# First squares of A issued later, pair 1's A groups sooner, one exchange of pair 2 later

## The chip, the cores and the metric

The kernel runs on one core of a Trainium2 chip. The metric is the device time of one execution in microseconds (us), as a median of several runs. TensorE is called PE (PEld where it loads weights), VectorE DVE, ScalarE ACT, GpSimd POOL. SyncE (SP) computes nothing: it issues nearly all DMAs and waits for semaphores, strictly in the order of its program. "SPq" in a row is that issuing.

## The reference

The input x has 8 sequences of 4096 rows with 192 columns. Each of 8 heads owns 24 columns and has 7 weights, which go through a softmax; a causal convolution over 7 rows is taken with them. Its result, 32768 rows of 192, goes through a gated feed-forward block with 1536 hidden units:

```
w = softmax(weight);  c[s] = sum_k w[head, k] * x[s - 6 + k]
g = c @ w_gate;  out = (g * sigmoid(g)) * (c @ w_val) @ w_out
```

## The kernel before, in words

**Tiling.** The 32768 rows are 64 blocks of 512 rows, two blocks to a pair, 32 pairs. The hidden units are 12 chunks of 128. The kernel's main loop goes over blocks and, inside, over chunks; its counter `at` numbers the chunks of the whole run, 0 to 767, so block n begins at chunk 12n and pair q at chunk 24q. For each chunk PE forms `gate` (L546) and `val` (L547) in PSUM, ACT applies the activation (L551, tile `silu`), DVE multiplies (L553, tile `h`), and PE multiplies `h` by the output weights (L558, tile `acc`). These output products run about a block behind: 8 matmuls ("pieces") per chunk. `gate` has two PSUM buffers, `val` three, `acc` one; ACT empties `acc` (L596) at two chunks of each block (in block 1 at chunks 16 and 22), and SP stores the result (L588). One output bank is summed in two passes. The second pass must start after the first, and this order is kept by an empty instruction on SP (`mark`, L443): PE's first piece of the second pass waits until SP has come to it.

**Convolution.** Block 0 and block 1 (pair 0) are convolved by PE in the opening, as matmuls with a banded matrix (L334). Block 1's are the calls `lateA` (chunks 2 and 4) and `lateC` (chunk 6); ACT copies the sums to `foldA1` and `foldC1`, and SP exchanges their lower and upper 64 partitions with two DMAs each (`exchange`, L657: `swapA` in chunk 4, `swapC` in chunk 6). Every chunk of block 1, the first (chunk 12) included, reads `foldA1`, `foldC1`, `swapA1` and `swapC1`, the last one last.

All later pairs are convolved by ACT, DVE and POOL. SP loads x as 32 by 32 squares (`emit_load`, L103) into `sqA` (channels 0 to 127, 1024 rows; parts 0 and 1, two DMAs each) and `sqB` (channels 128 to 191; parts 2 and 3). DVE transposes (`emit_turn`, L114) into `xtA` and `xtB`. A pair has three groups of 512 columns: g0 is the first half of A, g1 is B, g2 the second half of A. In a group ACT forms one product into a PSUM tile `run` (L473) and one or two more into tiles `t` (L466), DVE adds one or two taps (L483), POOL forms two or three products (L488), adds everything (L495) and writes the result `xc` (L501). SP then exchanges the halves of `xc` into `xs` with two DMAs (`swap`, L449 and L450), and PE reads both.

**Order.** It is written out by hand. `at_chunk(c, f)` puts f behind chunk c's own work; what is put at the same chunk runs in the order in which it was registered. `plan_group` puts one group's steps at given chunks: turn, start (ACT's `run`), ACT taps, DVE taps, POOL taps, join (POOL's adds and `xc`) and swap. For pair 1 these come from `PLAN["opening"]`, for pairs q from 2 on they are offsets to 24q from `PLAN["start"]`, `"swap"` and so on; the swaps of pair 2 stand at chunks 42 (g0), 35 (g1) and 53 (g2). Every engine executes its own instructions in this order, so a waiting instruction holds back all behind it on that engine.

Pair 1's squares are in four portions. Right after PE's first matmul of the band matrix (L310) SP issues the four loads of B and the first halves of A, four DMAs. The second halves of A follow at chunk 9.

Of the kernel before, what the change touches and what calls it, by code (L numbers as in the profile page):

```python
# [11 lines left out]
PLAN = dict(  # L12
    start=(-16, -24, -8), turn=-2,
    acts=((3, 5), (2, 4), (2, 4)), dves=(1, 3), pool=4, join=5, npool=(2, 2, 3),
    swap=(10, 11, 13),
    load=((2, -47), (3, -40), (0, -34), (1, -28)),
    opening=(
# [3 lines left out]
    ),  # L21
    gate=2, val=3, lead=4, third=(2, 11),
)
# [3 lines left out]
def kernel(  # L27
# [31 lines left out]
    n_pairs = NT // (2 * TB)  # L59
# [21 lines left out]

    def emit_load(q, part, half=None):
        head = q % ppb == 0
        if part == 2 and not half:
            squares[q, "A"] = headA if head else xpool.tile(
                [P, HIST + 2 * TB], fp32, tag="sqA", name="sqA"
            )
            squares[q, "B"] = headB if head else xpool.tile(
                [P, HIST + TB], fp32, tag="sqB", name="sqB"
            )  # L90
        for k in range(2):
            quad = 2 * (part % 2) + k
            if part < 2:
                tile_, t0, n, c = squares[q, "A"], 0, 2 * TB, SQ * quad
            else:
                tile_, t0, n, c = squares[q, "B"], TB * (part % 2), TB, P + SQ * k
            skip = HIST if head and t0 == 0 else 0
            row = q * 2 * TB + t0 - HIST + skip
            n = n // SQ + 1 - skip // SQ
            if half is not None:  # L100
                first = TB // SQ + 1
                skip, row, n = ((skip, row, first), (first * SQ, row + first * SQ, n - first))[half]
            nc.sync.dma_start(  # L103
                out=tile_[quad * SQ : (quad + 1) * SQ, skip : skip + n * SQ].rearrange("p (n c) -> p n c", c=SQ),
                in_=x_flat[row : row + n * SQ, c : c + SQ].rearrange("(n p) c -> p n c", p=SQ),
            )
# [9 lines left out]
    def sync_after(ins, earlier, why="one bank, two halves of the array"):  # L116
        tc.add_manual_dep(
            ins.ins,
            earlier.ins.name,
            mybir.DependencyInfo(mybir.DependencyClass.Sync, mybir.DependencyReason.DATA),  # L120
            reason=why,
        )
# [185 lines left out]
    def repeat(part, h0):  # L308
        bank = early[("hi", "lo")[part] + "AC"[h0 // HH]]
        return nc.tensor.matmul(  # L310
            bank[0:ROWS, 0 : HH * W], left[:, part, 0:ROWS],
            pick[:, h0 : h0 + HH, :].unsqueeze(2).to_broadcast([RT, HH, W // 8, 8]),
            start=True, stop=True,
        )
# [48 lines left out]

    if n_pairs > 1:
        sync_after(nc.sync.nop(), some, "squares after x")
        for part in (2, 3, 0, 1):
            emit_load(1, part, None if part > 1 else 0)
    repeat(1, 0)
    repeat(0, HH)
    repeat(1, HH)  # L370
# [244 lines left out]
    def at_chunk(c, f):  # L615
        todo.setdefault(c, []).append(f)

    def plan_group(q, g, turn, start, acts, dves, pool, join, swap):
        made = []
        if turn is not None:  # L620
            at_chunk(turn, lambda: emit_turn(q, g))

        def step(c, f):
            def run():
                if not made:
                    made.append(Group(q, g))
                f(made[0])

            at_chunk(c, run)

        ks = iter(range(1, K))
        step(start, lambda group: group.start_d())
        for k, c in zip(ks, acts):
            step(c, lambda group, k=k: group.act_tap(k))
        ks = list(range(1 + len(acts), K))
        for k, c in zip(ks, dves):
            step(c, lambda group, k=k: group.dve_tap(k, k == len(acts) + len(dves)))
        for k in ks[len(dves) :]:
            step(pool, lambda group, k=k: group.pool_tap(k))
        step(join, lambda group: group.join())  # L640
        step(swap, lambda group: group.swap())
# [39 lines left out]
    if n_pairs > 1:  # L681
        for part in (0, 1):
            at_chunk(9, lambda part=part: emit_load(1, part, 1))

    if n_pairs > 1:
        for g, plan in enumerate(PLAN["opening"]):
            plan_group(1, g, *plan)
    at_chunk(4, outA)
    for q in range(2, n_pairs):
        base = 2 * NCH * q  # L690
        for part, c in PLAN["load"]:
            c = {2: 14, 3: 15, 0: 17, 1: 21}[part] if q == 2 else base + c
            at_chunk(c, lambda q=q, part=part: emit_load(q, part))
        for g in range(3):
            c = base + PLAN["start"][g]
            plan_group(
                q, g, c + PLAN["turn"], c, [c + o for o in PLAN["acts"][g]],
                [c + o for o in PLAN["dves"][: 4 - PLAN["npool"][g]]],
                c + PLAN["pool"], c + PLAN["join"],
                c + PLAN["swap"][g],  # L700
            )


# [3 lines left out]
    for n in range(2 * n_pairs):  # L707
        block = Block(n)
        for j in range(NCH):
# [6 lines left out]
            half = src.done // (2 * NCH) - 1 if units and src.done % (2 * NCH) == 0 else None  # L716
# [82 lines left out]
```

## Time and profile before

| | us |
|---|---|
| median of 3 runs (lowest, highest) | 768.93 (768.78, 769.22) |
| the profiled execution's own time | 770.07 |
| its span | 768.3 |
| PE busy | 761.8 (99%) |
| POOL, DVE, ACT busy | 668.5, 658.4, 656.8 (87%, 86%, 85%) |
| SP's DMA row (q1), share of the 16 DMA engines | 38.5% |
| POOL's DMA row (q0: the weights), same share | 1.6% |

The profile is of one execution, whose time of 770.07 us is 1.77 us above its span. All times inside the run count from the start of the span. The granted clock of PE was 1.00. PE is busy 99% of the span, so a part of the run counts only where PE idles or is slowed; matmuls are pipelined, and PE can read as busy while it runs below its rate. A row of a timeline holds start, duration, engine, line and tiles; "xN" are N instructions merged.

### The profile page before, as it was taken

The numbers are of one execution on the slowest core, as the hardware profiler recorded it, in microseconds if no ns is written. First come the engines' busy times: TensorE is split into PE (matmuls) and PEld (weight loads), VectorE is DVE, ScalarE is ACT, GpSimd is POOL, SyncE is SP. The second block draws the span as 40 slices with busy tenths as digits, with TensorE's granted clock in tenths as the row PEclk, the third lists the DMA queues.
The fourth block names the chain that finished last, engine by engine and source line by source line (L and its number), as shares of the span: only waits on it lengthen the run. The fifth ranks groups of instructions, "written<-read, shape, count | busy, mean of one in ns | idle before, by whom it ended". The sixth has DMA issues, their size and how long they took to land.

```text
span 768.3 us, 28285 instructions
## 1 busy us (share of the span) xinstructions
PE 761.8 (99%) x11035; PEld 498.5 (65%) x11035; DVE 658.4 (86%) x1051; ACT 656.8 (85%) x1187; POOL 668.5 (87%) x650
## 2 busy tenths in 40 slices
PE   8999999999999999999999999999999999999998
PEld 3866666666666666666666666666666666666666
DVE  7888888888888888888888888888888888888875
ACT  6888888888888888888888888888888888888875
POOL 7999898888998888988889988889888899888850
PEclk9999999999999999999999999999999999999999
DMA  9543344434344433444443344334444334443211
GB/s 175 106 89 88 78 89 92 90 83 87 88 86 88 91 87 79 90 91 88 87 84 90 84 88 93 87 79 88 93 87 89 83 88 85 89 95 86 61 47 54
DMA packets 255280, 67.27 MB, mean 88 GB/s; under 512 B 207919, under 2 KB 255145, under 8 KB 255145
## 3 DMA queue, kind: packets, MB, share of 16 engines
q1 hardware_dynamic: 252041, 63.47, 38.5%
q0 software_dynamic: 2800, 1.77, 1.6%
q8 instruction: 86, 1.41, 0.8%
q14 instruction: 49, 0.40, 0.2%
q10 hardware_dynamic: 304, 0.22, 0.1%
HBM read 29.64 MB, written 25.17 MB: 71 GB/s over the span
## 4 chain that ended last, share of the span: by engine, by line
PE 96%; POOL 2%; DMA 1%; SPq 0%; issue 0%; ACT 0%; POOLq 0%
PE gate L546 60%; PE acc L558 32%; PE val L547 3%; DMA w_sb<-in_moe_w_val_dram 1%; POOL t L495 1%; DMA x_sb<-in_x_dram 0%; POOL xc L501 0%; PE acc L750 0%; POOL t L488 0%; SPq L450 0%; PE acc L334 0%; PE val L750 0%; PE run L750 0%; POOL x L229 0%; ACT silu L551 0%
## 5 line engine op out<-in xcount | busy, mean ns | idle before, releaser
L553 DVE TENSOR_TENSOR h<-silu,val 128x512 f16<-128x512 f16 x768 | 508.7, 680 | 100.5 <-ACT silu L551 69.8
L551 ACT ACTIVATE silu<-gate 128x512 f16<-128x512 f32 x768 | 452.9, 594 | 100.7 <-PE val L547 93.7
L495 POOL TENSOR_TENSOR t<-t,t 128x512 f32<-128x512 f32 x310 | 393.9, 1271 | 59.4 <-ACT t L466 38.1
L546 PE MATMUL gate<-xc,w_sb 64*128 64x512 f16 x1116 | 409.7, 376 | 0.0
L547 PE MATMUL val<-xc,w_sb 64*128 64x512 f16 x1116 | 409.7, 376 | 0.0
L558 PEld LDWEIGHTS <-h 64*128 64x128 f16 x6048 | 275.9, 94 | 141.3 <-SPq L443 1.7
L546 PE MATMUL gate<-xs,w_sb 64*128 64x512 f16 x1116 | 360.0, 376 | 0.0
L547 PE MATMUL val<-xs,w_sb 64*128 64x512 f16 x1116 | 360.0, 376 | 0.0
L558 PE MATMUL acc<-wo_sb,h 64*128 64x192 f16 x6048 | 356.4, 243 | 0.7 <-SPq L443 0.7
L546 PEld LDWEIGHTS <-w_sb 64*128 64x128 f16 x2340 | 212.3, 94 | 114.8 <-DMA w_sb<-in_moe_w_gate_dram 1.0
L547 PEld LDWEIGHTS <-w_sb 64*128 64x128 f16 x2340 | 208.3, 94 | 3.6 <-DMA w_sb<-in_moe_w_val_dram 1.7
L501 POOL TENSOR_TENSOR xc<-t,aD 128x512 f16<-128x512 f32 x93 | 118.1, 1270 | 7.3
L488 POOL TENSOR_SCALAR t<-xtA,wn 128x512 f32<-128x512 f32 x155 | 106.1, 696 | 0.7 <-DVE xtA L114 0.7
L466 ACT ACTIVATE t<-xtA,wn 128x512 f32<-128x512 f32 x124 | 88.5, 713 | 0.0
L596 ACT COPY o<-acc 128x384 f32<-128x384 f32 x126 | 60.4, 479 | 2.5
L488 POOL TENSOR_SCALAR t<-xtB,wn 128x512 f32<-128x512 f32 x63 | 43.0, 696 | 3.6 <-DVE xtB L114 3.6
L483 DVE SCALAR_TENSOR_TENSOR aD<-xtA,wn,run 128x512 f32<-128x512 f32 x62 | 45.9, 741 | 0.0
L466 ACT ACTIVATE t<-xtB,wn 128x512 f32<-128x512 f32 x61 | 43.5, 714 | 0.0
L473 ACT ACTIVATE run<-xtA,wn 128x512 f32<-128x512 f32 x62 | 42.5, 686 | 0.0
L114 DVE STREAM_TRANSPOSE xtA<-sqA 128x544 f32<-128x544 f32 (+1 forms) x48 | 34.6, 721 | 0.0
L483 DVE SCALAR_TENSOR_TENSOR run<-xtA,wn,run 128x512 f32<-128x512 f32 x31 | 23.2, 749 | 0.0
L483 DVE SCALAR_TENSOR_TENSOR run<-xtB,wn,run 128x512 f32<-128x512 f32 x31 | 23.2, 749 | 0.0
(112 smaller groups left out, 177.2 us busy)
## 6 DMA issues: line engine op xcount, KB each, us to landing
out_dram<-o SPq DMA_DIRECT2D x127, 192.0 KB, 2.0
sqA<-in_x_dram SPq DMA_DIRECT2D x92, 132.0 KB, 2.9
xs<-xc SPq DMA_DIRECT2D x186, 64.0 KB, 2.0
sqB<-in_x_dram SPq DMA_DIRECT2D x96, 68.0 KB, 2.3
headA<-in_x_dram SPq DMA_DIRECT2D x28, 128.0 KB, 2.6
headB<-in_x_dram SPq DMA_DIRECT2D x14, 68.0 KB, 2.3
headB<-in_x_dram SPq DMA_DIRECT2D x14, 64.0 KB, 2.0
w_sb<-in_moe_w_gate_dram POOLq DMA_DIRECT2D x3, 192.0 KB, 6.8
```

The costliest lines, as they stand in the source:

```text
L466: mul(parts[-1], *self.tap(k))
L473: nc.scalar.mul(self.aD, *self.tap(0))
L483: nc.vector.scalar_tensor_tensor(out=self.aD, in0=v, scalar=s, in1=run, op0=ALU.mult, op1=ALU.add)
L488: self.product(k, lambda t, v, s: nc.gpsimd.tensor_scalar(t, v, scalar1=s, scalar2=1.0, op0=ALU.mult, op1=ALU.mult), self.parts)
L495: nc.gpsimd.tensor_tensor(self.parts[0], self.parts[0], t, op=ALU.add)
L501: nc.gpsimd.tensor_tensor(xc, self.parts[0], self.aD, op=ALU.add)
L546: nc.tensor.matmul(g, w[0:DB, ca, f], a[0:DB, :], start=(i == 0), stop=(i == 2))
L547: nc.tensor.matmul(v, w[DB:P, cb, f], b[DB:P, :], start=(i == 0), stop=(i == 2))
L551: nc.scalar.activation(s, self.g.pop(j), AF.Silu)
L553: nc.vector.tensor_tensor(h, s, self.v.pop(j), op=ALU.mult)
L558: ins = nc.tensor.matmul(acc, self.h[j][r, ts(s, P)], wo_r[r, j, :], start=first and j == 0, stop=not first and j == NCH - 1, skip_group_c ...
L596: nc.scalar.copy(self.o[:, 2 * half : 2 * half + 2, :], self.acc[:, :, 0:D])
```

## The change

The change touches the first three pairs only. SP issues the first halves of pair 1's squares of A in chunk 4, behind block 1's first exchange (`outA`), and no longer in the opening. Pair 1's g0 has its steps one chunk sooner, all but the swap (chunk 20 as before). Its g2 is turned and started two chunks sooner, with ACT taps in chunks 20 and 22 (22 and 23 before), the DVE tap in 19 (21), POOL taps in 18 (20), join in 22 (23), and the swap in 31 as before. Pair 2's g2 is exchanged in chunk 56 (53 before).

```
     opening=(
-        (11, 13, (14, 15), (14, 15), 12, 15, 20),
+        (10, 12, (13, 14), (13, 14), 11, 14, 20),
         (2, 4, (8,), (4, 6), 4, 8, 14),
-        (18, 20, (22, 23), (21,), 20, 23, 31),
+        (16, 18, (20, 22), (19,), 18, 22, 31),
     ),
...
-        if part == 2 and not half:
+        if part == 2:
...
-        for part in (2, 3, 0, 1):
-            emit_load(1, part, None if part > 1 else 0)
+        for part in (2, 3):
+            emit_load(1, part)
...
     at_chunk(4, outA)
+    if n_pairs > 1:
+        for part in (0, 1):
+            at_chunk(4, lambda part=part: emit_load(1, part, 0))
...
-                c + PLAN["swap"][g],
+                c + PLAN["swap"][g] + (3 if (q, g) == (2, 2) else 0),
```

The entries of a plan are turn, start, ACT taps, DVE taps, POOL taps, join, swap. No instruction is added or taken away.

## The prediction

> **What bounds the kernel now.** I read the page first (PE busy 761.8 of 768.3 us), then the table of windows, cut at the first gate matmul of each block, to see where PE runs below its best. The columns are the stretch, its length, then busy time of PE, PEld, DVE, ACT and POOL.
>
> ```profile
> 8.50:20.90 12.40, 11.20 (x227) 5.74 (x228) 9.62 (x21) 8.59 (x17) 8.30 (x10) 1.00 1.16 168
> 20.90:33.06 12.16, 12.16 (x245) 11.80 (x243) 11.04 (x19) 9.88 (x19) 11.00 (x12) 1.00 0.66 119
> 33.06:45.07 12.01, 12.01 (x174) 8.08 (x170) 10.81 (x18) 10.90 (x21) 11.37 (x13) 1.00 0.35 76
> 45.07:57.65 12.58, 11.92 (x174) 7.85 (x170) 9.71 (x17) 10.73 (x20) 12.02 (x13) 1.00 0.50 103
> 57.65:69.38 11.73, 11.73 (x173) 7.43 (x170) 10.76 (x18) 9.89 (x19) 11.17 (x12) 1.00 0.30 70
> ```
>
> From block 4 on each block takes 11.73 us and PE waits for nothing. Blocks 1, 2 and 3 take 0.43, 0.28 and 0.85 more. So the change can give back 1.56 us there, and what PE idles in block 0. The waits of 8 to 60 us name the places.
>
> ```profile
> PE val L547 <- DMA w_sb<-in_moe_w_val_dram: 1.1, 2, 0.7
> DVE xtB L114 <- DMA sqB<-in_x_dram: 1.1, 1, 1.1
> POOL t L488 <- DVE xtA L114: 0.7, 2, 0.4
> PE acc L558 <- SPq L443: 0.7, 1, 0.7
> ```
>
> PE waits twice for value weights (0.44 us to 9.32, 0.69 to 13.82) and once, at 54.37, for SP's mark. The chain that ended last says why the mark was late.
>
> ```profile
> 51.14 1.28 POOL xc L501
> 52.43 0.47 SPq L449
> 52.96 1.22 SPq L450
> 54.37 0.51 PE acc L558 x8
> ```
>
> SP stood at the swap of pair 2's g0 until POOL had written `xc` at 52.41, issued two DMAs, and only then came to the mark. The second issue took 1.22, its twin at 42.06 only 0.59; one instruction packet of 16 KB ran from 52.88 to 53.80 in the DMA records, and SP's long issues elsewhere end about 0.4 after such a packet. POOL had worked without a gap since 30.04.
>
> **The moved loads: what they leave.** SP's timeline:
>
> ```profile
> 6.57 6.26 SPq L103 DMA_DIRECT2D sqA<-in_x_dram  x4
> 16.18 1.17 SPq L657 DMA_DIRECT2D swapA<-foldA  x2
> 17.64 1.93 SPq L657 DMA_DIRECT2D swapC<-foldC  x2
> 19.61 2.18 SPq L103 DMA_DIRECT2D sqA<-in_x_dram  x4
> ```
>
> The 6.26 us cost SP nothing: it then waits for ACT's `foldA1` until 16.16. What the loads cost others is DMA time beside the weights. Does the wait at 13.82 go? Its weights (issued 6.15) landed at 13.77, and the squares of B, which stand ahead of those of A in SP's queue, were awaited until 14.10. The last DMA engine to finish was thus still on B's squares, so A's had not come before the weights. I take 0, between 0 and -0.69. Even if the weights alone came sooner, `foldA1` would not: ACT's `run` ahead of it waits for `xtB`, hence for B's squares. POOL's weight issues (9.00, 9.63, 10.25) are not behind SP.
>
> **What they meet.** In chunk 4 the four loads stand behind `swapA` and ahead of `swapC`. SP is free of `swapA` at 17.35. Four such loads took 2.18 (the 19.61 row), so they would end at 19.57; but an instruction packet ran 17.60 to 18.55, and before, the `swapC` issue under it took 1.29 and ended 18.93. Now the second load is caught: it ends about 18.93, the fourth at 20.0. `swapC` is issued at 20.06 and 20.64 (0.53 and 0.59 each) in place of 17.64 and 18.97. It took 1.9 and 2.7 us to land; nothing queued, so 1.9: the second half lands at 22.55. PE wants it here:
>
> ```profile
> 21.55 0.27 PE L546 MATMUL gate<-swapC,w_sb 64*128 64x256 f16 x1
> 21.64 0.27 PE L547 MATMUL val<-swapC,w_sb 64*128 64x256 f16 x1
> ```
>
> PE waits from 21.64 to about 22.6: **+0.95**. Lower end 0: four loads at 0.31 (the shortest issue of that line) and 1.9 to land give 21.3. Upper end +2.4: a second load caught (+0.75) and 2.7 to land give 24.1. I take +0.95, built from the nearest rows. Behind `swapC`, A's second halves go from 21.3 to 23.5; next on SP is the mark of chunk 13 (23.2 before, 24.2 with PE's delay), so nothing else waits.
>
> **Pair 1's g0 one chunk sooner.** DVE's transpose (0.74) now stands behind `h` of chunk 10, which ended 21.64, and ahead of that of chunk 11. It waits for the fourth load, issued about 19.5; sets of such loads took 2.6 to 3.9 to land, so 22.1 to 23.4. I take 22.2, as the weights' traffic has ended by then. `h` 11 moves from 22.23 to about 23.55; PE needs it in chunk 13's last pieces at 22.9 before, 23.85 now. Covered by 0.3; without PE's wait it would cost some 0.6. POOL's first tap of g0 comes at 23.0, as before (22.99). ACT's gain is in chunk 15:
>
> ```profile
> 25.51 0.73 ACT L466 ACTIVATE t<-xtA,wn 128x512 f32<-128x512 f32 x1
> 26.12 0.48 ACT L596 COPY o<-acc 128x384 f32<-128x384 f32 x1
> 26.48 1.11 ACT L551 ACTIVATE silu<-gate 128x512 f16<-128x512 f32 x2
> ```
>
> The tap held back the copy of `acc` and with it `silu` 16 (ended 27.10); gate 18, whose buffer that frees, started at 27.16, and chunk 17 took 1.24 us instead of 0.98. The second tap now lies in chunk 14, the copy starts when its sum is complete: **-0.26** (between -0.26 and 0).
>
> **Pair 1's g2 two chunks sooner.** In chunks 22 to 24 ACT had a copy (31.64), two taps (0.71 at 32.83, 0.72 at 33.92) and pair 2's `run` (0.70 at 35.01), so chunks 24 to 26 took 1.02, 1.10 and 1.09 us, 0.27 over 0.98 each. One tap goes from chunk 23 to 20, where ACT has room: **-0.27** (between -0.27 and 0). DVE's transpose at chunk 16 meets squares that landed by 25.5 to 26. POOL loses the idle 0.28 before 30.04, so its later work is 0.28 sooner: pair 2's `xc` at 52.1.
>
> **The mark in block 3.** PE comes to it at 53.52 (54.37 less block 3's 0.85) plus 0.95 - 0.26 - 0.27 = 53.94. SP issues the swaps from 52.15; the instruction packet follows PE and starts near 53.3, after the second issue began. SP is past the mark by 53.6. Nothing waits: **-0.85**. If POOL gained nothing and the issue were caught again, SP would be free at 54.37 as before, and the total would be 0.
>
> **Pair 2's g2 swap** moves on SP from 63.10 to behind chunk 55's mark, about 65.8. It lands 2.0 later (3.2 in the worst row, 42.06 to 45.25), at 67.8 to 69.0; PE reads it in chunk 60's second step, 69.6. Cost 0, as the landing is hidden; without cover it would be some tenths. The load of pair 4's B behind it has till chunk 70.
>
> **Sum.** 0.95 - 0.26 - 0.27 - 0.85 = -0.43 us. The profiled execution's 770.07 would become 769.64; it lies 1.14 above the median of the runs, which becomes 768.5. With the ends of the first term alone it is 767.55 to 769.95.
>
> **The rivals.**
>
> *The exchange is hidden anyway.* If SP gets the loads out in 1.4 us, PE does not wait at 21.64, but then `h` 11 and SP's marks in chunk 13 lose their cover: -1.38 and some 0.4 back, 767.95. For it: issues of 0.31 exist on that line. Against: those of this size took 0.46 to 0.58.
>
> *Weights and B's squares come sooner.* While both rows were at work, SP's row and the weights' row shared the engines: in 9 to 11 us the DMA view gives the weights' row 97.3% and SP's 37.8%. If all that is ahead of `foldA1` comes 0.69 sooner, the exchange does too: 767.8, and with the exchange hidden 767.2. The Trainium skill, "DMA: Bandwidth & Descriptors", section "Queues, rings and completion order", says that each DMA engine takes turns between the queue rows that have work, packet by packet, which would speak for this rival; the trace agrees that both rows move at once. Against it stands that B's squares are ahead of A's in the same row and landed after the weights.
>
> *Slower: the squares land late for the turn.* DVE then stands at the transpose, `h` 11 behind it, POOL's whole chain behind that. POOL's chain comes later by the landing less 22.4 (22.15 + 0.28 of gap that it can absorb). Landing at 23.4, the 3.9 row, gives up to +0.97, 769.9. PE's own path (-0.43, plus the landing less 22.45, by which `h` 11 is late) crosses zero at 22.9, and from 24.0 POOL's makes it slower by 0.2%: the loads of the opening took 7.4 (median) and 8.3, and one at 24.5 gives +2.1, 771.0. For it: POOL's output weights are landing until 19.9. Against: the DMA share falls from 1.38 (10 to 15 us) to 0.45 (20 to 25).
>
> **How the numbers follow.** A measurement of this kernel tells about 0.2%, 1.54 us, from no change. Chances: forecast 0.56, all within that; exchange hidden 0.14, within; weights sooner 0.12, 0.08 of it over 0.2% (with the exchange hidden as well); squares late 0.18, 0.14 of it over 0.2%. Together faster 0.08, same 0.78, slower 0.14. The range takes in the hidden exchange with weights sooner and the squares late up to a landing of 23.8 or so: 767.2 to 770.3.
>
> **What would show it.** Right: in SP's timeline four `sqA` issues from 17.4 and `swapC` from about 20; PE waiting for `swapC` near 21.6 to 22.6; no wait of PE for L443 at 54; chunk 17 at 0.98; blocks 2 and 3 at 11.73 to 11.8; later blocks 11.73. Wrong: PE's wait for value weights at 13.8 gone, DVE idle before `xtA` until 24 or later, or a new wait of PE for `xs` at chunk 60.

## The result and the profile after

| | before | after |
|---|---|---|
| median of 7 runs each, same chip (us) | 769.22 (768.66 to 770.12) | 772.83 (770.56 to 774.35) |
| the profiled execution's own time | 770.07 | 772.83 |
| its span | 768.3 | 771.0 |
| chunk 12 begins | 20.90 | 19.92 |
| block 1, block 2, block 3 | 12.16, 12.01, 12.58 | 16.84, 11.73, 11.73 |

The ratio is 1.0043, with a 95% interval of 1.0033 to 1.0053: the change makes the kernel slower by 0.43%, and the time is outside the range of the prediction. The two spans differ by 2.73 us. By stages, after less before: the start of block 0 -0.11, block 0 -0.87, block 1 +4.68, block 2 -0.28, block 3 -0.85, all the rest +0.16.

The table of windows of the kernel after, cut at the ends of block 0, of chunk 12 and of chunk 15, and at the ends of blocks 1, 2 and 3 (columns: stretch, length, busy PE, PEld, DVE, ACT, POOL, granted clock, DMA share, GB/s; the last line is a stretch inside chunks 13 to 15):

```profile
8.39:19.92 11.53, 10.89 (x225) 5.93 (x227) 9.54 (x21) 8.57 (x17) 8.33 (x10) 1.00 1.15 164
19.92:24.26 4.34, 1.51 (x25) 1.01 (x22) 2.06 (x4) 1.65 (x3) 3.39 (x5) 1.00 0.54 92
24.26:29.21 4.95, 4.95 (x73) 4.65 (x70) 3.27 (x5) 2.88 (x5) 2.61 (x3) 0.66 0.28 52
29.21:36.76 7.55, 7.55 (x157) 7.55 (x154) 6.07 (x11) 6.44 (x13) 6.52 (x7) 1.00 0.73 135
36.76:48.49 11.73, 11.73 (x173) 10.55 (x170) 10.75 (x18) 10.39 (x20) 11.18 (x14) 1.00 0.33 74
48.49:60.22 11.73, 11.73 (x173) 9.92 (x170) 9.72 (x17) 10.62 (x20) 11.17 (x11) 1.00 0.53 110
24.62:28.03 3.41, 3.41 (x42) 3.11 (x38) 1.76 (x4) 1.89 (x4) 1.73 (x2) 0.50 0.13 27
```

Blocks 2 and 3 are at the 11.73 of all later blocks. Two things cost the time, both in block 1. Chunk 12 takes 4.34 us, in which PE works for 1.51. Then PE reads as busy throughout, and still chunks 13 to 15 take 4.95, where the kernel before needs 3.28, because the granted clock is 0.50 for 3.41 us.

Three waits of 8 to 70 us that the kernel before did not have (waiting line, what it waited for, total, times, longest):

```profile
PE gate L546 <- DMA swapC<-foldC: 1.8, 1, 1.8
PE val L547 <- DMA swapC<-foldC: 1.0, 1, 1.0
DVE xtA L114 <- DMA sqA<-in_x_dram: 0.9, 1, 0.9
```

PE waits for `swapC` twice, and the wait for SP's mark (L443) is gone. SP's timeline shows what stood ahead of `swapC`:

```profile
15.33 1.18 SPq L657 DMA_DIRECT2D swapA<-foldA  x2
16.55 2.98 SPq L103 DMA_DIRECT2D sqA<-in_x_dram  x4
19.63 1.11 SPq L657 DMA_DIRECT2D swapC<-foldC  x2
20.78 2.86 SPq L103 DMA_DIRECT2D sqA<-in_x_dram  x4
```

And PE's timeline shows what that does to chunk 12, and then the slow clock:

```profile
20.55 0.27 PE L547 MATMUL val<-swapA,w_sb 64*128 64x256 f16 x1
22.61 0.27 PE L546 MATMUL gate<-swapC,w_sb 64*128 64x256 f16 x1 [1.79 <-DMA swapC<-foldC]
23.92 0.27 PE L547 MATMUL val<-swapC,w_sb 64*128 64x256 f16 x1 [1.04 <-DMA swapC<-foldC]
...
25.83 0.42 PE L546 MATMUL gate<-foldA,w_sb 64*128 64x256 f16 x1
```

PE idles 1.79 and 1.04 us, 2.83 in all, with one matmul between. A matmul of 256 columns takes 0.27 before that, and 0.42 in the stretch behind it. The chain that ended last goes through the second transfer itself:

```profile
19.84 0.25 SPq L657
20.14 3.73 DMA swapC<-foldC
23.92 0.26 PE val L547
```

### The profile page after: what moved, and what is told of

Its sections match the earlier page's. It is cut to its first block, busy times and chain, and to the rows that moved or that the text cites. A ratio compares the mean times of both kernels' runs of the same rounds, so it can differ in the third digit from the quotient of the medians.

```text
span 771.0 us, 28285 instructions
## 1 busy us (share of the span) xinstructions
PE 763.0 (99%) x11035; PEld 649.2 (84%) x11035; DVE 658.7 (85%) x1051; ACT 663.0 (86%) x1187; POOL 667.7 (87%) x650
## 4 chain that ended last, share of the span: by engine, by line
PE 98%; DMA 1%; POOL 0%; ACT 0%; issue 0%; SPq 0%; POOLq 0%
PE val L547 46%; PE acc L558 32%; PE gate L546 20%; DMA w_sb<-in_moe_w_val_dram 1%; DMA swapC<-foldC 0%; PE acc L753 0%; PE acc L334 0%; PE val L753 0%; PE run L753 0%; POOL w_sb L158 0%; ACT silu L551 0%; POOL mask L211 0%; ACT o L772 0%; POOL plain L202 0%; SPq L657 0%
## 5 line engine op out<-in xcount | busy, mean ns | idle before, releaser
L558 PE MATMUL acc<-wo_sb,h 64*128 64x192 f16 x6048 | 449.6, 243 | 0.0
L558 PEld LDWEIGHTS <-h 64*128 64x128 f16 x6048 | 398.9, 94 | 41.2 <-issue 1.2
L547 PEld LDWEIGHTS <-w_sb 64*128 64x128 f16 x2340 | 212.8, 94 | 67.5 <-issue 2.4
L546 PEld LDWEIGHTS <-w_sb 64*128 64x128 f16 x2340 | 212.9, 94 | 3.1 <-DMA w_sb<-in_moe_w_gate_dram 0.6
```

The costliest lines, as they stand in the source:

```text
L546: nc.tensor.matmul(g, w[0:DB, ca, f], a[0:DB, :], start=(i == 0), stop=(i == 2))
L547: nc.tensor.matmul(v, w[DB:P, cb, f], b[DB:P, :], start=(i == 0), stop=(i == 2))
L558: ins = nc.tensor.matmul(acc, self.h[j][r, ts(s, P)], wo_r[r, j, :], start=first and j == 0, stop=not first and j == NCH - 1, skip_group_c ...
```

## The experiments

**Theory 1:** the loss comes from the four loads of A alone; behind `swapA` they are ahead of `swapC` in SP's queue. Rivals: the sooner steps of pair 1 cost it (DVE's transpose waits for squares), or nothing but the sooner end of block 0 (0.98) makes PE come too soon. **Theory 2:** `swapC` lands late, and not 1.9 us after its issue, because an instruction packet (16 KB in the DMA records, here 21.73 to 22.69) holds a DMA engine. There are 86 of these in the run and 22070 matmuls and weight loads, so one for about 257 instructions of PE; this is why they are taken for fetches of PE's instructions. **Theory 3:** PE's gap lowers its clock, and this costs a further 1.6 us.

### The two halves of the change apart

The loads alone, with plan and swap as before (this edit and the next are against the kernel after):

```
     opening=(
-        (10, 12, (13, 14), (13, 14), 11, 14, 20),
+        (11, 13, (14, 15), (14, 15), 12, 15, 20),
         (2, 4, (8,), (4, 6), 4, 8, 14),
-        (16, 18, (20, 22), (19,), 18, 22, 31),
+        (18, 20, (22, 23), (21,), 20, 23, 31),
...
-                c + PLAN["swap"][g] + (3 if (q, g) == (2, 2) else 0),
+                c + PLAN["swap"][g],
```

> The kernel before with one part of the change: the four loads of A's first halves in chunk 4, behind swapA and ahead of swapC. Pair 1's plan and pair 2's swap stay as before. Theory 1 (the second exchange comes late, PE idles for it and then runs at half clock): block 0 some 0.9 us shorter (no wait for value weights at 13.8), block 1 some 4.7 longer, no wait for the mark in block 3 (-0.85), so about 772.3 us, a ratio of 1.003 to 1.005 to before. Rival (the sooner turn is what costs: DVE held by the squares, h of chunk 11 late): with the turn at chunk 11 as before the loss is gone, 768.3 or less.

Measured: 773.85 us against 769.64 for the kernel before, ratio 1.0048 (1.0034 to 1.0061). PE's waits from 14 to 60 us:

```profile
PE gate L546 <- DMA swapC<-foldC: 1.8, 1, 1.8
PE acc L558 <- SPq L443: 0.5, 1, 0.5
PE val L547 <- DMA swapC<-foldC: 0.5, 1, 0.5
```

The same wait, the same 3.41 us at clock 0.50 (24.38 to 27.79), and the wait for the mark still there. The loads alone carry the loss. Block 0 ended at 20.67 here, about as late as in the kernel before (20.90), so a sooner PE is not needed for it.

The plan and the later swap alone, with the loads back in the opening:

```
-        if part == 2:
+        if part == 2 and not half:
...
-        for part in (2, 3):
-            emit_load(1, part)
+        for part in (2, 3, 0, 1):
+            emit_load(1, part, None if part > 1 else 0)
...
-    if n_pairs > 1:
-        for part in (0, 1):
-            at_chunk(4, lambda part=part: emit_load(1, part, 0))
```

> The kernel before with the other part alone: pair 1's g0 and g2 sooner and pair 2's g2 swap at chunk 56; the loads stay in the opening. Theory 1: PE waits for value weights at 13.8 as before (0.69), swapC lands before PE wants it, chunk 17 and chunks 24 to 26 at 0.98 us (-0.26, -0.27), no or less wait for the mark in block 3 (up to -0.85): 767.8 to 768.3. Rival (the sooner turn costs): slower than before, 770 or more.

Measured: 768.51 against 769.64, ratio 0.9982 (0.9973 to 0.9991). No wait of PE is left from 14 to 70 us. Blocks 0 to 3 by the table of windows:

```profile
9.33:20.14 10.81, 10.55 (x225) 5.68 (x226) 9.59 (x21) 8.66 (x17) 7.65 (x9) 1.00 1.21 174
20.14:32.11 11.97, 11.97 (x247) 11.95 (x244) 11.01 (x19) 10.54 (x20) 11.41 (x13) 1.00 0.60 110
32.11:43.84 11.73, 11.73 (x173) 8.96 (x170) 10.75 (x18) 10.34 (x20) 11.18 (x12) 1.00 0.43 89
43.84:55.57 11.73, 11.73 (x173) 9.66 (x170) 9.72 (x17) 10.62 (x20) 11.24 (x12) 1.00 0.52 108
```

So the plan gives what its steps said, 12.16, 12.01 and 12.58 becoming 11.97, 11.73 and 11.73. The same kernel measured again:

> Pair 1's plan and pair 2's later swap with the loads left in the opening, timed once more in five rounds, as the version that should beat both kernels. Theory 1: 0.9975 to 0.9990 of the kernel before. Rival (its gain was within the noise of the rounds): 0.9995 to 1.0005.

768.63 against 769.49, ratio 0.9990 (0.9981 to 0.9998). Both intervals lie under 1: this version is faster than the kernel before, by 0.1 to 0.2%, some 1 us, and so faster than the kernel after as well.

And without pair 2's later swap:

```
-                c + PLAN["swap"][g] + (3 if (q, g) == (2, 2) else 0),
+                c + PLAN["swap"][g],
```

> The kernel before with pair 1's plan alone; the loads stay in the opening and pair 2's g2 is exchanged in chunk 53 as before. Theory 1 (the later swap of pair 2 is hidden either way): the time of the run with plan and later swap, 768.5, within 0.3. Rival (at chunk 53 SP waits at this swap for POOL and holds the mark behind it): 0.4 to 0.8 more, 769.0 or over.

768.83 against 769.46, ratio 0.9995 (0.9984 to 1.0005). The blocks are those of the run above within 0.02 us. The swap's place makes no difference that these runs can tell.

### Both kernels again

> The kernel before once more, for one more profile of its opening. Theory 1: with the squares of A in the opening the value weights of chunks 4 to 7 land at 13.0 to 13.8, about 1 us later than in the runs without them (11.9 to 12.8); PE waits for them if its block 0 begins near 8.5 and hardly if it begins near 9.3. Rival (the squares have nothing to do with it): they land at 12.0.

> The changed kernel once more, on the same chip as the next run. Theory 1: as before, swapC's second half lands 3 us or more after its issue, at 23.4 to 24.2, PE idles 2.3 us or more for it and a half-clock stretch of 3.41 us follows; 772 to 773.5. Rival (the profile of it was a chance): landing by 22.6, clock 1.00 throughout, 770.

The kernel before had no wait for value weights at 13.8 this time: block 0 began at 9.60 instead of 8.50, the weights landed at 13.36, and chunk 12 began at 20.80, within 0.10 of the first profile. So an early start of block 0 and that wait offset each other here: begun 1.10 later, block 0 ended 0.10 sooner.

The kernel after took 772.02 against 769.49, ratio 1.0034 (1.0021 to 1.0046). Its table of windows for blocks 0, 1 and 2:

```profile
8.30:19.48 11.18, 10.82 (x225) 5.55 (x226) 9.79 (x21) 8.67 (x17) 8.37 (x10) 1.00 1.18 172
19.48:34.72 15.24, 12.35 (x246) 11.85 (x243) 11.20 (x19) 10.67 (x20) 12.54 (x13) 1.00 0.54 100
34.72:46.45 11.73, 11.73 (x173) 10.55 (x170) 10.76 (x18) 10.39 (x20) 11.18 (x14) 1.00 0.43 89
```

PE idled 2.89 us for `swapC` (1.85 and 1.04), as much as in the first profile, but the clock stayed at 1.00, and block 1 took 15.24 instead of 16.84. The same kernel with nearly the same gaps, with and without the slow stretch: block 1 differs by 1.60 us, chunks 13 to 15 by 1.67 (3.28 here).

The mean granted clock of each run is on record, and one slow stretch of 3.41 us in 771 lowers it to 0.998. Of the 15 runs of the kernel after, nine have 0.997 or 0.998 and lie at 772.63 to 774.35 (median 773.27); six have 1.00 and lie at 770.45 to 771.66 (median 770.93). So the clock parts them. The medians are 2.34 apart, more than the slow stretch cost in the profile; what makes the rest stays open. (Of 80 runs of the kernel before, two have 0.998 as well, and they are no longer than the others.) Even with the clock at 1.00 the kernel is 1.4 to 1.7 us slower than the kernel before (769.49 and 769.22).

### The gap filled: does it cost clock?

Twelve matmuls on zeros, whose result is not used, ahead of chunk 12's products with `swapC`:

```
-            for g, v, lo, hi in passes:
+            for k, (g, v, lo, hi) in enumerate(passes):
...
+                    if (self.n, j, k, i) == (1, 0, 1, 2):
+                        keep_busy(12)
...
+    def keep_busy(n):
+        spare = tpool.tile([P, TB], fp32, tag="run", name="run")
+        for _ in range(n):
+            nc.tensor.matmul(
+                spare[:, :].rearrange("p (r c) -> p r c", c=P), zeros,
+                zeros.unsqueeze(1).to_broadcast([P, SUBS, P]), start=True, stop=True,
+            )
```

> The changed kernel with 12 matmuls of zeros on PE (some 2.6 us) between chunk 12's products with swapA and those with swapC, into a bank of PSUM that nobody reads: PE does something while it waits. Theory 1: the wait for swapC ends at the same time (about 22.6 and 23.9), but the clock is not halved for the 3.41 us after it: 1.7 less than the changed kernel, about 771.1. Rival (the halved clock costs nothing, since ACT, DVE or POOL would be late anyway): 772.8 as the changed kernel.

Measured: 771.65 against 769.64, ratio 1.0024 (1.0015 to 1.0034). The new matmuls in PE's timeline, and block 1 in the windows:

```profile
20.57 2.76 PE L618 MATMUL run<-zeros 128*128 128x512 f16 x12
```

```profile
19.75:34.79 15.04, 14.98 (x257) 12.87 (x254) 11.21 (x19) 10.67 (x20) 12.55 (x13) 1.00 0.58 107
```

The idle time is gone, the delay stays, and the clock is 1.00; block 1 costs what it costs in the run without the slow stretch. The profile is as theory 3 wants it. The ten runs agree: all have a clock of 1.00, against six of 15 for the kernel after, so it is the idle time that costs the clock. The median is no better than that kernel's runs at full clock (770.93), as the products with `swapC` still come late.

### The loads at other places

Ahead of the first exchange instead of behind it: the loads stand in chunk 2, behind an empty instruction of SP that waits for `lateA`'s first sum.

```
+        ins = halves(g, late["sum"][:, g, :])
+        if g == 0 and n_pairs > 1:
+            sync_after(nc.sync.nop(), ins, "squares after block 1's first sum")
+            for part in (0, 1):
+                emit_load(1, part, 0)
...
-        for part in (0, 1):
-            at_chunk(4, lambda part=part: emit_load(1, part, 0))
```

> The changed kernel, but the four loads stand in SP's idle stretch: in chunk 2, behind an empty SP instruction that waits for the end of lateA's first sum on PE (about 12.0 us), so ahead of both exchanges. Theory 1: the weights of chunks 4 to 7 have landed by then (no PE wait at 13.8), both exchanges are on time, PE never idles, the clock stays at 1.00: block 0 11.5, blocks 1 to 3 11.75 to 11.9, so 766.6 to 767.3, faster than both kernels. Rival (the weights came sooner by chance): PE waits at 13.8 again, 767.6 or more.

Measured: 770.30 against 769.64, ratio 1.0012 (0.9998 to 1.0025). The gain did not come. SP's timeline (the exchange is L661 in this kernel):

```profile
12.11 3.80 SPq L103 DMA_DIRECT2D sqA<-in_x_dram  x4
16.00 3.26 SPq L661 DMA_DIRECT2D swapA<-foldA  x2
19.36 1.18 SPq L661 DMA_DIRECT2D swapC<-foldC  x2
```

Issued from 12.11 on, the squares landed only at 19.35 to 19.96, after POOL's output weights (18.86). Beside them the two issues of `swapA` took 3.26 us instead of 1.18 (an instruction packet, 17.32 to 18.26, fell on them too; the two causes are not told apart), so `swapC` was issued about as late as in the kernel after. PE waited 1.93 for it, from 21.47 to 23.39 (and 0.6 for SP's mark later), and the clock was 0.50 from 22.92, while PE still waited, to 26.33. Three of the ten runs, the profiled one among them, have a clock of 0.997 or 0.998; the seven at 1.00 lie at 769.28 to 770.42, about where the kernel before does.

Behind the second exchange, in chunk 6:

```
-            at_chunk(4, lambda part=part: emit_load(1, part, 0))
+            at_chunk(6, lambda part=part: emit_load(1, part, 0))
```

> The changed kernel with the four loads in chunk 6, behind the second exchange and not ahead of it. Theory 1: swapC is on time (issued 16.8 to 18.5, landed by 20.5), so the 2.8 us and the half clock go; the squares land 1 to 2 us later than in the changed kernel, 22.3 to 23.8, DVE stands at the turn of chunk 10 and h of chunk 11 comes at 23.7 to 25, for which PE waits 1 to 2 us, short of what halves the clock: 768.3 to 770.5. Rival (the turn that waits for squares is the cause of the loss): as slow as the changed kernel or slower, 772.5 or more.

Measured: 772.06 against 769.46, ratio 1.0033 (1.0021 to 1.0046). `swapC` landed at 19.34 and 20.02, and PE did not wait for it. The squares now landed at 24.30. The profiled run is again one of those with a lowered clock, three of seven. The waits of 18 to 30 us and the clock behind them:

```profile
DVE xtA L114 <- DMA sqA<-in_x_dram: 3.5, 1, 3.5
PE acc L558 <- DVE h L553: 3.3, 1, 3.3
```

```profile
26.71:30.13 3.42, 3.42 (x42) 2.85 (x38) 2.94 (x5) 2.43 (x5) 3.26 (x3) 0.50 0.50 92
```

DVE stood 3.45 at the transpose with `h` 11 behind it, and PE 3.31 for `h` 11. This is the mechanism of the prediction's slower rival, here made by another place of the loads. One queue, two customers: with the loads ahead, `swapC` is late; with them behind, the transpose is.

The loads where the change has them, `swapC` issued by ACT:

```
-    def exchange(out, fold):
+    def exchange(out, fold, queue=nc.sync):
...
-        exchange(swapC1, foldC1)
+        exchange(swapC1, foldC1, nc.scalar)
```

> The changed kernel, but swapC's two DMAs are issued by ACT, right behind its copy of foldC1, and so are no longer behind the four loads on SP. Theory 1 (the place of the second exchange in SP's queue is the cause): swapC is issued near 16.5 to 18 and has landed by 20.5, PE's wait of 2.8 us and the half clock go; ACT loses some 1.1 us of issuing in chunk 6, and DVE's turn still waits for the squares until about 21.4, so h of chunk 11 costs PE a few tenths: 767.3 to 769.0. Rival (it is the loads' own traffic beside the exchange, or the turn that waits for them): 771 or more.

Measured: 770.47 against 769.46, ratio 1.0014 (1.0004 to 1.0023). No wait for `swapC`, block 1 at 11.82, clock 1.00. Two new waits of PE took the place (14 to 60 us):

```profile
PE gate L546 <- ACT silu L551: 1.4, 1, 1.4
PE acc L558 <- SPq L443: 0.8, 1, 0.8
```

ACT's own timeline shows the first: the two issues hold it for 1.60 us and `silu` 7 stands behind them.

```profile
17.03 0.37 ACT L666 CAST foldC<-acc 128x256 f16<-128x256 f32 x1
17.43 1.60 ACTq L657 DMA_DIRECT2D swapC<-foldC  x2
19.13 1.08 ACT L551 ACTIVATE silu<-gate 128x512 f16<-128x512 f32 x2 [1.74 <-PE val L547]
```

### The landing of `swapC`

In the kernel after, `swapC`'s two issues ended at 20.09 and 20.73; the second, which started at 20.14, landed at 23.88. The trace records 16 completions for each. Fourteen of the second half's had come by 22.05:

```
first half   15 by 21.58, the last 22.57
second half  14 by 22.05, then 22.79 and 23.88
instruction packet of PE (16 KB): 21.73 to 22.69
```

To move that packet against the exchange, small matmuls on zeros were put into the opening, 40 in one kernel, 88 in another:

```
+    for _ in range(40):
+        nc.tensor.matmul(early["idle"][:, 0:16], zeros, zeros[:, 0:16], start=True, stop=True)
```

> The changed kernel with 40 small matmuls of zeros (128x16) on PE in the opening, while it waits for weights: 80 instructions more, so that PE's instruction packet of 16 KB, which ran 21.73 to 22.69 while swapC was under way, comes at another time (18 to 20). Theory 2 (that packet holds up one DMA engine, and the last sixteenth of the exchange with it): swapC's halves land 1.9 to 2.4 after their issue, the second by 22.6, PE waits 1 to 1.9 us in place of 2.8; 1 us or more under the changed kernel of this call, 1.5 more if the clock is not halved. Rival (the exchange is late by the squares ahead of it in the DMA rings): landing at 23.4 to 24.2 again, time as the changed kernel.

> As the run with 40 small matmuls, now with 88 (176 instructions more), which costs about 2.2 us in the opening and should put one of PE's instruction packets near 15 us and the next behind PE's wait for swapC, so that none runs while the exchange is under way. Theory 2 (the packet holds up one DMA engine): all 16 completions of swapC's second half come within 0.6 us of each other and 1.7 to 2.3 after its issue, where in the changed kernel one of 16 came 1.1 behind the others; PE's wait ends about 1 us sooner after the issue than there. Rival (the late sixteenth has another cause, such as A's squares ahead of it): one completion is again 1 us or more behind. The time itself says little, as the small matmuls cost theirs: 771 to 774.

With 40: 771.10 against 769.49, ratio 1.0026 (1.0014 to 1.0037). The packet ran from 20.99 to 21.87, still within the exchange, and the halves landed 3.2 and 2.9 after their issue. By this run nothing is told apart. With 88: 774.12, ratio 1.0062 (1.0045 to 1.0078); the new matmuls and what they delay cost more than all else, block 0 being 13.44, so the total says nothing, but the landing does. The packet was over at 21.86, before `swapC`'s issues at 22.37 and 22.88. The tile's row, in the kernel with 88, in the kernel after, and in the kernel before:

```profile
DMA to landing us min/median/max: 1.8/1.8/1.9
```

```profile
DMA to landing us min/median/max: 2.9/3.3/3.7
```

```profile
DMA to landing us min/median/max: 1.9/2.3/2.7
```

With 88, all 16 completions of each half came within 0.21 us, and no wait of PE for `swapC` is listed. This speaks for theory 2, and the other traces bear it out. In the run with the loads in chunk 6 no packet fell on `swapC`, and it took 1.81 and 1.90; in the runs of the plan, with no load between the exchanges, a packet from 17.3 to 18.5 did, and it took 2.4 to 3.2. So a packet goes with a late exchange where no load stands ahead of it, and loads ahead without a packet (the run with 88) do not make it late. The swaps of the later pairs say the same: in the kernel after, from 34 us on, the 36 transfers `xs<-xc` with a packet within 1.8 us of their issue took 3.15 to land (median; up to 4.04), the 122 without one 1.96 (nine in ten under 2.06). None of this shows that the engine with the packet and the engine with the late completion are one.

## Why the prediction was wrong

Two steps failed: the time that `swapC` takes to land, taken as 1.9 us and measured at 3.73, and the price of PE's wait, taken as its length with no term for the clock. Set against the terms of its sum, in the profile's own time:

| step | predicted | measured |
|---|---|---|
| weights' wait, up to chunk 12 | 0 | chunk 12 begins 0.98 sooner |
| exchange behind the loads | +0.95 | 2.83 of idle time |
| PE's clock behind that | not in the sum | 1.60 to 1.67 in the first profile, 0 in the second |
| g0 sooner (chunk 17) | -0.26 | chunk 17 at 0.99, as told |
| g2 sooner (chunks 24 to 26) | -0.27 | 0.98 each, block 2 -0.28 |
| mark in block 3 | -0.85 | block 3 -0.85 |
| pair 2's swap later | 0 | 0 |

**The exchange: right mechanism, wrong size.** The prediction had `swapC` issued at 20.06 and 20.64; it was 19.63 and 20.14. Four loads took 2.98 of SP's time with the first one, not the second, caught by an instruction packet (16.59 to 17.55). What failed is the next step, "nothing queued, so 1.9", the landing at 22.55. It landed at 23.88, 3.73 after its issue. The upper end of the term (24.1) reached that far only with a second load caught as well. The profile before had both landings, 1.9 and 2.7, and the lower one was taken without asking where the next instruction packet would fall. The packets follow PE's progress (87 in place of 86 with 88 more matmuls), so a trace tells roughly where one falls; the prediction used this for the mark in block 3 but not for the landing.

**Chunk 12 came sooner, which made the same landing worse.** PE wanted `swapC` at about 20.66, 0.98 sooner than 21.64. The wait grew by this 0.98, and the two cancel: the end of chunk 12 is set by the landing, whenever PE comes. The step "weights' wait 0" was thus off in this execution, since the wait at 13.82 was gone and block 0 ended sooner, but that did not move the end. Whether the moved loads bring the weights sooner stays open. With A's squares in the opening the weights landed at 12.70 to 13.77 (five profiles), without them at 11.86 to 13.55 (nine); the means are 13.2 and 12.5 but the spreads overlap, and the start of block 0 alone varies from 8.1 to 10.5 between executions. The rival "weights sooner" was thus no gain even where its condition held, because its other half, the exchange sooner by as much, did not come: `swapA` was issued 0.85 sooner (15.33 for 16.18), but `swapC` landed 1.33 later than forecast.

**The clock: a missing term.** The prediction priced PE's wait as its length. A gap of 2 to 3 us cost up to 1.60 more. The Trainium skill, "TensorE: Matmul & The Clock Gate", Part 1 "The HAM clock gate", says that the gate watches windows of 4096 cycles (3413 ns) that run freely, and halves the clock behind an idle one. The trace agrees on the length of the slow stretch, 3.41 us each time, and on a grid: in all four profiles that have the stretch, it begins a whole number of 3.41 us (4, 5 or 6) behind the clock's first rise, which lies at 4.1 to 10.7. It does not agree that the window must be idle. These are the window ahead of the slow stretch in the kernel after, and the two windows on which the gaps fell in its second profile, where the clock stayed:

```profile
21.21:24.62 3.41, 0.97 (x17) 0.79 (x18) 1.65 (x3) 1.18 (x2) 2.54 (x4) 1.00 0.50 84
```

```profile
18.18:21.59 3.41, 2.20 (x30) 1.40 (x26) 1.87 (x4) 1.76 (x4) 2.56 (x3) 1.00 0.62 108
21.59:25.00 3.41, 1.73 (x33) 1.55 (x34) 1.84 (x3) 1.44 (x3) 2.63 (x3) 1.00 0.45 70
```

PE idled 2.44 of the 3.41 us in the first, where the clock then fell, and 1.21 and 1.68 in the others. So the place of the grid can account for one kernel having the slow stretch in one execution and not in another. It does not give a limit: in the other three profiles with a slow stretch PE idled 2.33 (loads alone), 2.40 (chunk 6) and only 1.60 (chunk 2) in the window ahead of it. The Trainium skill's advice on the same page ("Why this matters for your kernels"), no gaps above some 3 us, is too mild for this kernel: the slow stretch came behind 1.79 and 1.04 us with a matmul of 0.27 between, and 1.45 us into a single gap of 1.93.

**The squares and the turn.** DVE waited 0.89 for squares that landed at 21.43, sooner than the 22.2 taken; `h` 11 ended at 22.87 and PE, held up itself, did not wait for it. The slower rival, the squares late, did not happen in the change itself; the loss came from the forecast's own term and from the clock.

**The plan's terms were right.** Run alone, plan and swap came to 1.13 and 0.86 us below the kernel before (medians, measured twice), where -0.26, -0.27 and -0.85 make -1.38. Block 1 kept 0.24 over 11.73, so the first of these is nearer -0.2. SP's timeline in the run of plan and swap alone shows why the mark no longer waits:

```profile
50.94 0.47 SPq L449 DMA_DIRECT2D xs<-xc  x1
51.46 0.59 SPq L450 DMA_DIRECT2D xs<-xc  x1
```

The second issue took 0.59 instead of 1.22, and SP was past the mark before PE came.

**The sum as measured.** Block 1 with the plan alone takes 11.97. The 16.84 of the kernel after is that plus 2.83 of idle time, 1.60 by the clock and 0.44 that no row names (the run at full clock has 0.38 of it; 0.42 lies in chunk 12, which without its idle time takes 1.51, and 1.09 with the plan alone). Against these 4.87 stand the 0.98 by which chunk 12 began sooner, and the 1.32 of the plan's terms in blocks 1 to 3 (0.19, 0.28 and 0.85); with +0.16 in later blocks this makes 2.73, the difference of the spans. Seen from the forecast, whose sum was -0.43: chunk 13 began 1.33 later than it said (24.26, where 21.98 in the kernel before and the 0.95 make 22.93), the clock took 1.67, and the later blocks 0.16, which makes 2.73 again. So the clock's missing term is the larger of the two errors in this profile; in the one at full clock, where chunk 13 began at 23.89, the landing's is left.

## What to carry to other kernels

In a queue that issues in order, "behind one transfer" is "ahead of the next": before a load is moved, look for what stands behind its new place, and price it by its slowest completion, from rows in which an instruction packet fell on it. A wait of 2 to 3 us on TensorE is not worth its length only; look at the granted clock for some microseconds behind it, and count up to 1.67 us more, as here. And where a change has several parts, the useful ones may be had without the one that costs: here the sooner plan needed no moved load.

## What the runs showed of the hardware that was not expected

- One fetch of PE instructions (a packet of 16 KB, 0.9 to 1.9 us long) goes with long DMA issues on SP and ACT: 1.6 for two on ACT, 2.98 for four loads that took 2.18 elsewhere. Where a transfer is under way, one or two of its 16 completions come 1 to 2 us late: `xs<-xc` took 3.15 with a packet and 1.96 without (medians in the kernel after).
- PE's clock fell to 0.50 for 3.41 us behind, or within, idle time of 1.9 to 3.3 us in some executions, and stayed at 1.00 behind 2.89 in another. In the window of 3.41 us ahead of the fall PE had idled 1.60 to 2.44 us, not all of it.
- While POOL's output weights were on their way, loads on SP's row moved hardly at all for a time: issued from 12.11 on, they landed at 19.35 and later. From 14 to 16 us SP's row had 8 packets and the weights' row 818.
